# Fixed queue orders in the gradient pass, larger weight pieces at the hand-over, and the final parameter step in blocks

## Chip, cores and metric

One Trainium2 chip, one core. The time is the device time of one execution in microseconds, from three runs; the profile is of one more execution. PE is the matmul engine, DVE the vector engine, ACT the scalar engine, POOL GpSimd and SP the sync engine, which here only issues DMAs. ACT and POOL issue DMAs too, and each engine works through its own instructions in order: a DMA that has to wait on a semaphore holds up what stands behind it.

## What is computed

A layernormed input goes through a state-space convolution and is multiplied by the silu of a SwiGLU feed-forward; the kernel gives the output and the gradients by all inputs, L = 2048 rows, D = 576 channels, N = 128 states, F = 4608 hidden columns.

```python
xn = _layernorm(x)
s = _A_ref(xn, A_A_re, A_A_im, A_B_re, A_B_im, A_C_re, A_C_im, A_log_dt, A_Dskip)   # SSM convolution
h = silu(xn @ w1) * (xn @ w3); g = silu(h @ w2)
out = x + s * g
_out, _vjp = jax.vjp(_f, A_u, ..., B_w1, B_w3, B_w2); _grads = _vjp(grad_out)
```

out_0 is the output, out_1 the gradient by x, out_2 to out_9 those by the SSM parameters (out_8 by log_dt, 576 numbers), out_10 and out_11 by w1 and w3, out_12 by w2.

## The kernel before

A forward part (hidden columns, SSM, output) fills scratch tensors in DRAM: the gate values G, the up values U and spectra of the SSM (Q, PZ). `backward` then runs the **gradient pass**: 18 groups of 256 hidden columns (`FG`). For each, `phase6_load` brings two rows of w2 into one of four buffers on POOL (L1224), transposes them on SP to `w2T`, loads `gg_n` (G, L1229) and `h_n` (U, L1230) on POOL and prepares Silu (L1234) and its derivative (L1236) on ACT. `phase6_group` multiplies the output gradient by w2 (`ph`, L1259; its PSUM tiles are freed by ACT's copies `gh`, L1262) in four parts, with stages "h1" and "h3" after the second and fourth, stores GU and GG with SP, and goes on to the weight gradients: `phase6_grad2` (out_12, two a group, copies L1292) and `phase6_grad13` (out_10, out_11, copies L1309). The next group's tiles are loaded while a group runs; `gg_n` and `h_n` have two buffers each. A scheduler places the instructions on each engine by priorities (`at`).

Beside this, the SSM's backward convolution runs until about 1390 us; from group 11 on (`GP`) **parameter steps** (`param_step`, 72 of them, each half a chunk of 16 channels) are spread between the stages: SP loads `qT` and `gz`, ACT loads `pz` (L995), PE makes eight small matmuls into `et_ps` (three buffers), DVE multiplies (L1010) and reduces (L1013) into `S_all`. From there SP's order is the order of the code (`chain`).

At the **hand-over** the transposed weights w1 and w3 (36 blocks of 128 columns each) come in by SP as pieces, five transposes a piece (`load_piece`): 14 blocks of each early, the rest into buffers that the gradient pass gives back, then the transposed GG and GU rows (`acts`) of tiles 0 and 1. `phase6_inputs` makes the input gradient of 16 row tiles, 144 matmuls `px` each (L1348), adds on DVE (`gx`, L1355), and `ln_bwd_tile` goes back through the layernorm and stores out_1 (L1385). The remaining parameter steps stand at fixed stops in these tiles. `phase5_final` then turns `S_all` into out_2 to out_8, five chunks of channels: four PE transposes, some thirty DVE operations over 128 elements, and stores; out_8 goes out by elements at the end (L1096, L1098).

## Time and profile before

| | us |
|---|---|
| median of three runs | 2099.3 (2097.39 to 2102.25) |
| profiled execution / its span | 2097.32 / 2095.3 |
| PE busy | 1802.7 (86%) |
| DVE busy | 1401.2 (67%) |
| ACT busy | 881.0 (42%) |
| POOL busy | 278.9 (13%) |
| mean granted PE clock | 0.946 |

Stages in the span: the forward part up to about 840 us, the gradient pass to about 1640, the hand-over to about 1745, the input-gradient tiles to 2042, and the rest to 2095. The mean shares say little of a stage; a row of busy time for one stretch does. In rows of the time line a bracket holds the idle time of the engine ahead of the group and what ended it; "SPq" is SP's queue.

### The profile page before, as it was taken

The page shows a single profiled execution, that of the slowest core. Times are in us where ns is not written, and L with a number is a line of the kernel's source. Part 1 is how long each engine was busy: PE and PEld are TensorE (multiplying, and loading weights), DVE is VectorE, ACT ScalarE, POOL GpSimd, SP SyncE. Part 2 cuts the span into 40 slices and gives each one's busy share as a digit, 9 for nine tenths or more (in the row PEclk, how much of TensorE's full clock was granted, in tenths as well). Part 3 has the DMA queues.
Part 4 walks back from the last instruction along what each step waited for, and adds up shares of the span by engine and source line. Part 5 has one row for each costly group of instructions (what it writes and reads, how often), then busy time and mean ns, then how long its engine had stood idle before and what let it go on. Part 6 is the DMA issues. An engine that isn't in the chain of part 4 may idle for free. (4 is left out here: it accounts for less than half of the span.)

```text
span 2095.3 us, 40471 instructions
## 1 busy us (share of the span) xinstructions
PE 1802.7 (86%) x16538; PEld 1315.6 (63%) x16538; DVE 1401.2 (67%) x2283; ACT 881.0 (42%) x1612; POOL 278.9 (13%) x426
## 2 busy tenths in 40 slices
PE   1789999999997998899999998987797667998990
PEld 1444545455553676778787887876686545776880
DVE  7546565566884555396975979376697745787847
ACT  2967777775553111565656555445343100000000
POOL 5002222211113111111111111111110000000000
PEclk9999999999998999899999999998898888999995
DMA  3588777766659976547463756678789979999950
GB/s 79 209 310 284 263 261 254 268 236 234 204 171 256 222 188 176 178 149 204 144 189 113 204 160 203 180 180 202 195 216 186 209 141 208 203 217 192 214 129 20
DMA packets 625769, 411.24 MB, mean 196 GB/s; under 512 B 434160, under 2 KB 565360, under 8 KB 620976
## 3 DMA queue, kind: packets, MB, share of 16 engines
q1 hardware_dynamic: 566816, 272.26, 53.1%
q0 software_dynamic: 27792, 109.14, 15.5%
q10 hardware_dynamic: 30976, 27.27, 4.8%
q8 instruction: 129, 2.11, 0.4%
q14 instruction: 56, 0.46, 0.1%
HBM read 130.65 MB, written 185.65 MB: 151 GB/s over the span
## 5 line engine op out<-in xcount | busy, mean ns | idle before, releaser
L1348 PEld LDWEIGHTS <-acts 128*128 128x128 bf16 x2304 | 227.6, 100 | 93.6 <-DMA acts<-GU_dram 17.7
L1307 PEld LDWEIGHTS <-xn_bf 128*128 128x128 bf16 x2304 | 225.4, 98 | 33.9 <-issue 6.9
L1259 PE MATMUL ph<-w2T,goT 128*128 128x256 bf16 x1440 | 188.7, 285 | 66.2 <-ACT gh L1262 61.7
L1010 DVE TENSOR_TENSOR pr_q<-et_ps,pz 128x1024 f32<-128x1024 f32 x144 | 176.2, 1223 | 99.3 <-PE et_ps L1005 91.5
L1259 PEld LDWEIGHTS <-goT 128*128 128x128 bf16 x1440 | 144.7, 102 | 93.9 <-issue 65.4
L1348 PE MATMUL px<-wT,acts 128*128 128x288 bf16 x1408 | 181.9, 289 | 9.9 <-DMA wT<-in_B_w_dram 9.7
L1013 DVE TENSOR_REDUCE S_all<-pr_q 128x32 f32<-128x1024 f32 x144 | 175.3, 1217 | 3.5
L763 PE MATMUL pg<-wmB_w,xnT 128*128 128x512 bf16 x576 | 167.6, 382 | 3.8 <-ACT g_t L771 1.9
L763 PEld LDWEIGHTS <-xnT 128*128 128x128 bf16 x1152 | 104.7, 97 | 105.2 <-issue 19.3
L1288 PE MATMUL pgw<-go_o,h_n 128*128 128x288 bf16 x1152 | 158.3, 294 | 10.4 <-ACT gw L1292 10.4
L818 PE MATMUL po<-w2g,hc 128*128 128x288 bf16 x1152 | 148.6, 291 | 15.1 <-DMA w2g<-in_B_w_dram 14.9
L763 PE MATMUL pu<-wmB_w,xnT 128*128 128x512 bf16 x576 | 159.3, 380 | 0.5 <-ACT u_t L772 0.5
L767 ACT ACTIVATE s_t<-pg 128x512 bf16<-128x512 f32 x144 | 86.3, 599 | 145.1 <-PE pu L765 113.0
L1371 ACT ACTIVATE t<-gx 128x576 f32<-128x576 f32 x16 | 10.9, 683 | 315.0 <-DVE gx L1355 315.0
L818 PEld LDWEIGHTS <-hc 128*128 128x128 bf16 x1152 | 113.1, 99 | 47.1 <-issue 16.1
L1309 ACT CAST gw<-pgw 128x256 bf16<-128x256 f32 x144 | 54.2, 377 | 208.2 <-PE pgw L1307 188.1
L1288 PEld LDWEIGHTS <-h_n 128*128 128x128 bf16 x1152 | 115.3, 101 | 41.9 <-issue 11.2
L1348 PE MATMUL px<-wA,acts 128*128 128x288 bf16 x896 | 122.8, 297 | 20.4 <-DMA acts<-GU_dram 16.0
L1307 PE MATMUL pgw<-gu_n,xn_bf 128*128 128x256 bf16 x1152 | 133.2, 275 | 5.7 <-ACT gw L1309 4.4
L1307 PE MATMUL pgw<-gg_n,xn_bf 128*128 128x256 bf16 x1152 | 130.2, 273 | 0.0
L487 ACT ACTIVATE cs_k<-et_ps 128x512 bf16<-128x512 int16 x216 | 116.0, 640 | 6.6 <-PE et_ps L486 6.5
L777 POOL DMA_DIRECT2D G_dram<-g_t x72 | 52.6, 730 | 496.1 <-ACT g_t L771 477.2
(302 smaller groups left out, 3383.2 us busy)
## 6 DMA issues: line engine op xcount, KB each, us to landing
G_dram<-g_t POOLq DMA_DIRECT2D x72, 256.0 KB, 3.3
U_dram<-u_t POOLq DMA_DIRECT2D x72, 256.0 KB, 4.4
H_dram<-h_t SPq DMA_DIRECT2D x72, 256.0 KB, 3.4
Q_dram<-q_k SPq DMA_DIRECT2D x36, 512.0 KB, 3.2
gg_n<-G_dram POOLq DMA_DIRECT2D x18, 1024.0 KB, 5.8
h_n<-U_dram POOLq DMA_DIRECT2D x18, 1024.0 KB, 8.9
GU_dram<-gu_n SPq DMA_DIRECT2D x36, 512.0 KB, 4.3
GG_dram<-gg_n SPq DMA_DIRECT2D x36, 512.0 KB, 8.6
```

The source lines that it names most:

```text
L487: nc.scalar.activation(out=CS[:, :, o:o + 256], in_=pt[:].bitcast(I16)[:, :, 0::2], func=ACT.Sin, scale=6.283184 / 2 ** 16)
L763: nc.tensor.matmul(pt[:], lhsT=xnT[:, c, ts], rhs=wm[w][:, c, :], start=(c == 0), stop=False)
L767: nc.scalar.activation(out=s_t[:, :, q, :], in_=pgv, func=ACT.Silu)
L777: nc.gpsimd.dma_start(out=dst[fb * ng:(fb + 1) * ng, :, i0:i0 + NT, :].rearrange("g p t f -> p g (t f)"), in_=src[:].rearrange("p g t f -> ...
L818: nc.tensor.matmul(po_[:, pi_, 0:pw], lhsT=hc[:, fi, :], rhs=w2[fi][:, po:po + pw], start=(fi == 0), stop=(fi == FT - 1))
L1010: nc.vector.tensor_tensor(out=pr[:].rearrange("p r k e -> p r (k e)"), in0=T[h][:].rearrange("p k z d a -> p (k z d a)")[:, None].to_broad ...
L1013: nc.vector.tensor_reduce(out=self.S_all[:, :, d0:d0 + 4], in_=pr[:].rearrange("p r k (d a) -> p (r k) d a", d=4), op=ALU.add, axis=AX.X)
L1259: self.pe_last = nc.tensor.matmul(ph[j][:, k, :].rearrange("p (a f) -> p a f", f=P), lhsT=lw, rhs=rh, start=(n == 0), stop=(n == nfull))
L1288: self.pe_last = nc.tensor.matmul(pgw[pi_][:, 0:pw], lhsT=hn[:, tt, fl * P:(fl + 1) * P], rhs=go_o[:, tt, po:po + pw], start=(tt == 0), st ...
L1307: self.pe_last = nc.tensor.matmul(pw_[:, 0:FG], lhsT=self.xn_bf[:, tt, c * P:(c + 1) * P], rhs=nat[:, tt, :], start=(tt == 0), stop=(tt == ...
L1309: nc.scalar.copy(out=gw[:, c], in_=pw_[:, 0:FG])
L1348: self.pe_last = nc.tensor.matmul(px[pi_][:, 0:pw], lhsT=act[:, ai, fi, :], rhs=wT[ai][n][2][:, fi - f0, po:po + pw], start=(fi == 0 and a ...
```

## The change

Fixed orders: `after` makes an instruction follow the last one of its chain; `gp` does so for POOL's DMAs and `sc` for ACT's operations in the gradient pass. The w2 rows are loaded by SP, both rows of a group into one of two buffers, one group ahead; `h_n` is loaded two groups ahead at "h3"; Silu is issued at "h1", its derivative and the products at "h3"; the small remainders of out_10 and out_11 (`tail`) go behind the next `gg_n` load. The `pz` load is issued half a chunk earlier, apart from `qT` and `gz`.

Hand-over: 15 blocks of w1 and 13 of w3 come early, the rest in pieces of seven (and one of two); the four grad2 of the last two groups run ahead of the last grad13, with the piece loads between; GG of tile 1 is loaded ahead of the last two pieces, GU behind them, and step loads of the last group are held back (`hold`) until then. `phase6_inputs` takes the blocks in the order of the pieces and has steps at other stops, none in tile 0.

Final step: `phase5_blocks` takes five blocks of 64 (the last 32) channels of each half, in pieces that run at the stops as soon as the block's chunks are summed, with loads and stores on POOL, out_8 by elements after block 3 and block 4. `ln_bwd_tile` uses the `pr_q` buffer in place of its own.

```diff
+    def after(self, key, fn):
+        prev = self.last.get(key)
+        if prev is None:
             ins = fn()
         else:
-            with self.tc.issue_after(self.sp_last.ins):
+            with self.tc.issue_after(prev.ins):
                 ins = fn()
...
+    def sp(self, fn):
+        return self.after("sp", fn) if self.chain else fn()
+
+    def gp(self, fn):
+        return self.after("gp", fn)
+
+    def sc(self, fn):
+        return self.after("sc", fn)
 
...
         if dg == 1 and ch + 2 < nch:
-            self.loaded[ch + 2] = self.param_loads(ch + 2)
+            if self.hold is None:
+                self.loaded[ch + 2] = self.param_loads(ch + 2)
+            else:
+                self.hold.append(ch + 2)
         self.half += 1
+
+    def param_flush(self):
+        hold, self.hold = self.hold, None
+        for ch in hold:
+            self.loaded[ch] = self.param_loads(ch)
+            if (ch - 1) * 2 + 1 <= self.half:
+                self.param_load_p(ch)
+
...
-    def phase5_final(self, out, big, S_all, ps2):
...
+    def phase5_step(self, done):
+        if self.final_rows is None or done >= self.final_rows:
+            self.final_rows = next(self.final, 10 ** 6)
+
+    def phase5_blocks(self):
...
+        for j, c0 in enumerate(range(0, H, 64)):
+            R = min(64, H - c0)
+            v = slice(0, 2 * R)
...
+            sv = self.S_all[:].rearrange("p r (h c) -> p r h c", h=2)[:, :, :, c0:c0 + R]
+            sm = fp.tile([P, 4, 2, R], FP32, name="ST")
+            tt(out=sm[:, 0:2], in0=sv[:, 1:4:2], in1=sv[:, 4:8:2], op=ALU.subtract)
+            tt(out=sm[:, 2:4], in0=sv[:, 0:4:2], in1=sv[:, 5:8:2], op=ALU.add)
...
+            for k in range(2):
+                tt(out=Q[v, k, 0:2], in0=X[v, 2 + k:3 + k].to_broadcast([2 * R, 2, N]), in1=X[v, 0:2], op=ALU.mult)
+            tt(out=W[v, 0], in0=Q[v, 0, 0], in1=Q[v, 1, 1], op=ALU.subtract)
+            tt(out=W[v, 1], in0=Q[v, 0, 1], in1=Q[v, 1, 0], op=ALU.add)
+            yield 0
+            pt = self.ps_T.tile([P, 4, N], FP32, name="et_ps")
+            with self.tc.issue_after(self.pe_last.ins):
+                for k in range(4):
+                    nc.tensor.transpose(pt[v, k, :], sm[:, k].rearrange("p h c -> p (h c)"), self.ident_f[:])
...
+            yield 0
...
+            for k in range(2):
+                tt(out=Q[v, k], in0=ST[v, 2 * k:2 * k + 1].to_broadcast([2 * R, 4, N]), in1=X[v, 0:4], op=ALU.mult)
+            tt(out=O[v, 0:2], in0=Q[v, 0, 0:4:2], in1=Q[v, 1, 1:4:2], op=ALU.subtract)
+            nc.vector.scalar_tensor_tensor(out=O[v, 2:4], in0=Q[v, 0, 1:4:2], scalar=-1.0, in1=Q[v, 1, 0:4:2],
+                                           op0=ALU.mult, op1=ALU.subtract)
+            for k, on in enumerate(("out_6", "out_4", "out_7", "out_5")):
+                for h in range(2):
+                    nc.gpsimd.dma_start(out=aps[on][H * h + c0:H * h + c0 + R, :], in_=O[R * h:R * h + R, k])
+            yield 0
...
+            for k in range(2):
+                tt(out=Q[v, k, 0:2], in0=W[v, k:k + 1].to_broadcast([2 * R, 2, N]), in1=ST[v, 1:4:2], op=ALU.mult)
+            tt(out=ST[v, 1], in0=Q[v, 0, 0], in1=Q[v, 1, 1], op=ALU.subtract)
+            nc.vector.scalar_tensor_tensor(out=ST[v, 3], in0=Q[v, 0, 1], scalar=-1.0, in1=Q[v, 1, 0],
+                                           op0=ALU.mult, op1=ALU.subtract)
...
+            for k, (a, b) in enumerate(((ST[v, 1:4:2], X[v, 4:6]), (ST[v, 0:1], W[v, 0:1]), (ST[v, 2:3], W[v, 1:2]))):
+                nc.vector.tensor_tensor_reduce(out=Q[v, 1, 2:4] if k == 0 else Q[v, 1, 2:3], in0=a, in1=b, scale=1.0, scalar=0.0,
+                                               op0=ALU.mult, op1=ALU.add, accum_out=acc[v, k:k + 1])
+            tt(out=acc[v, 0:1], in0=acc[v, 0:1], in1=acc[v, 1:2], op=ALU.add)
+            tt(out=self.gl_bf[v, j:j + 1], in0=acc[v, 0:1], in1=acc[v, 2:3], op=ALU.subtract)
...
+            for ai, n in ((0, 15), (1, 13)):
+                wT.append((ai, 0, n, wA.tile([P, n, D], BF16, name=f"wA{ai}")))
...
-                nxt = self.phase6_load(gi + 1, T0 + TG * gi, TG, wp, inp) if gi + 1 < NG else None
+                lastg = gi == NG - 1
+                nxt = self.phase6_load(gi + 1, T0 + TG * gi, TG, wp, inp) if not lastg else None
+                prep = nxt[-1] if nxt else iter(())
+                if lastg:
+                    self.tail()
...
                 for stage in self.phase6_group(gi, cur, elp, gwp, ps_h, ps_gw):
-                    if stage in ("h1", "h3") and gi < NG - 2:
-                        w2(gi, stage == "h3")
-                    if stage == "h1" and gi == NG - 1:
-                        self.load_piece(wT, inp, "gg_n", ((0, FA, 7),))
-                        self.load_piece(wT, inp, "gu_n", ((1, FA, 7),))
-                        self.load_piece(wT, wp, "w2T", ((0, FA + 7, 2),))
+                    if stage in ("h1", "h3"):
+                        next(prep, None)
+                        if gi < NG - 2:
+                            w2(gi, stage == "h3")
+                        if stage == "h3" and gi + 2 < NG:
+                            self.phase6_load_h(gi + 2, T0 + TG * gi, inp)
+                    if stage == "h1" and lastg:
+                        self.load_piece(wT, inp, "gg_n", 0, 15, 7)
+                        self.load_piece(wT, inp, "gu_n", 1, 15, 7)
+                        self.load_piece(wT, wp, "w2T", 1, 13, 2)
                     if stage == "stored":
                         c = gi - GP
                         if 0 <= c < cfg.DT:
...
+                        if c in (1, 3):
+                            step()
...
-                            for fl in range(2):
-                                w2(gi - 1, fl)
+                            for g in (NG - 2, NG - 1):
+                                for fl in range(2):
+                                    w2(g, fl)
                                 step()
-                            self.load_piece(wT, wp, "w2T", ((1, FA + 7, 2),))
-                            self.load_piece(wT, inp, "h_n", ((0, FA + 9, 3), (1, FA + 9, 3)))
-                    elif gi >= GP:
+                                if g == NG - 2:
+                                    self.load_piece(wT, inp, "h_n", 1, 22, 7)
+                                else:
+                                    self.load_piece(wT, inp, "h_n", 0, 22, 7)
+                            acts.append(self.load_acts(1, (0,)))
+                    elif gi >= GP and not (lastg and stage in ("out_10", "end")):
                         step()
                 cur = nxt
-            for fl in range(2):
-                w2(NG - 1, fl)
-                step()
-            self.load_piece(wT, inp, "gg_n", ((0, FA + 12, 7),))
-            self.load_piece(wT, inp, "gu_n", ((1, FA + 12, 7),))
-            self.load_piece(wT, inp, "h_n", ((0, FA + 19, 3), (1, FA + 19, 3)))
-            for w in wT:
-                w.sort(key=lambda part: part[0])
-            acts.append(self.load_acts(1))
+            step()
+            self.load_piece(wT, inp, "gg_n", 0, 29, 7)
+            self.load_piece(wT, inp, "gu_n", 1, 29, 7)
+            self.load_acts(1, (1,), acts[1])
+            self.param_flush()
             ffn.close()
-            self.phase6_inputs(T2, TX, wT, acts)
-            while self.half < 2 * (D // 16):
-                self.param_step()
+            self.phase6_inputs(T2, TX, wT, acts, pool)
...
+    def phase6_load_h(self, gi, T, inp):
+        self.at(T)
+        hn = inp.tile([P, self.cfg.LT, self.FG], BF16, name="h_n")
+        self.gp(lambda: self.nc.gpsimd.dma_start(out=hn[:], in_=self.U_dram[gi]))
+        self.hn[gi] = hn
...
-            fi = gi * nfl + fl
-            w2r = self.w2rows[fi % len(self.w2rows)]
-            nc.gpsimd.dma_start(out=w2r[:, 0:D], in_=aps["B_w2"][fi * P:(fi + 1) * P, :])
-            self.nat_transpose(w2T[:, fl], w2r[:])
+            self.nat_transpose(w2T[:, fl], self.w2rows[gi % 2][:, fl])
+        if (gi + 1) * FG < cfg.F:
+            self.w2row_load(gi + 1)
         gg = inp.tile([P, LT, FG], BF16, name="gg_n")
-        hn = inp.tile([P, LT, FG], BF16, name="h_n")
         gu = inp.tile([P, LT, FG], BF16, name="gu_n")
-        nc.gpsimd.dma_start(out=gg[:], in_=self.G_dram[gi])
-        nc.gpsimd.dma_start(out=hn[:], in_=self.U_dram[gi])
+        self.gp(lambda: nc.gpsimd.dma_start(out=gg[:], in_=self.G_dram[gi]))
+        if self.tail:
+            self.tail()
+        self.tail = None
+        hn = self.hn[gi]
+        return w2T, hn, gg, gu, self.phase6_prep(hn, gg, gu)
+
+    def phase6_prep(self, hn, gg, gu):
+        nc, LT = self.nc, self.cfg.LT
         quarters = [slice(s * LT // 4, (s + 1) * LT // 4) for s in range(4)]
-        self.at(T + 0.4 * TG)
         for sl in quarters:
-            nc.scalar.activation(out=gu[:, sl, :], in_=gg[:, sl, :], func=ACT.Silu)
+            self.sc(lambda: nc.scalar.activation(out=gu[:, sl, :], in_=gg[:, sl, :], func=ACT.Silu))
+        yield
         for sl in quarters:
-            nc.scalar.activation(out=gg[:, sl, :], in_=gg[:, sl, :], func=ACT.Derivative_silu)
+            self.sc(lambda: nc.scalar.activation(out=gg[:, sl, :], in_=gg[:, sl, :], func=ACT.Derivative_silu))
         for sl in quarters:
             nc.vector.tensor_tensor(out=gg[:, sl, :], in0=gg[:, sl, :], in1=hn[:, sl, :], op=ALU.mult)
             nc.vector.tensor_tensor(out=hn[:, sl, :], in0=gu[:, sl, :], in1=hn[:, sl, :], op=ALU.mult)
-        return w2T, hn, gg, gu
...
-                stops = (6, 18, 30) if 0 < i and i % 2 == 0 else (8, 22)
-                for n in range(len(wT[0])):
-                    f0, f1 = wT[0][n][:2]
-                    for fi in range(f0, f1):
-                        for ai in range(2):
-                            for pi_, (po, pw) in enumerate(pieces):
-                                self.pe_last = nc.tensor.matmul(px[pi_][:, 0:pw], lhsT=act[:, ai, fi, :],
-                                                                rhs=wT[ai][n][2][:, fi - f0, po:po + pw],
-                                                                start=(fi == 0 and ai == 0),
-                                                                stop=(fi == FT - 1 and ai == 1))
-                        if fi in stops:
-                            self.param_step()
+                stops = () if i == 0 else (14, 38, 62) if i % 2 == 0 else (20, 50)
+                for n, (ai, fi, w) in enumerate(steps):
+                    for pi_, (po, pw) in enumerate(pieces):
+                        self.pe_last = nc.tensor.matmul(px[pi_][:, 0:pw], lhsT=act[:, ai, fi, :], rhs=w[:, po:po + pw],
+                                                        start=(n == 0), stop=(n == len(steps) - 1))
+                    if n in stops:
+                        self.param_step()
+                        self.phase5_step(self.half // 2)
```

On POOL, around the load of `gg_n` for a late group (before): out_dram<-gw rows are stores of weight gradients, w2r the w2 rows.

```order
L1293 DMA out_dram<-gw_19380 128x576
L1312 DMA out_dram<-gw_19412 128x4x256
L1312 DMA out_dram<-gw_19502 128x4x256
L1224 DMA w2r_10820<-in_B_w_dram 128x576
L1321 DMA out_dram<-gw13t 64x256
L1322 DMA out_dram<-gw13t 64x256
L1229 DMA gg_n<-G_dram 128x4096
L1224 DMA w2r_10821<-in_B_w_dram 128x576
L1293 DMA out_dram<-gw_19765 128x576
```

The same place on POOL after the change:

```order
L1356 DMA out_dram<-gw_19398 128x576
L1270 DMA h_n<-U_dram 128x4096
L1376 DMA out_dram<-gw_19428 128x4x256
L1376 DMA out_dram<-gw_19522 128x4x256
L1286 DMA gg_n<-G_dram 128x4096
L1388 DMA out_dram<-gw13t 64x256
L1389 DMA out_dram<-gw13t 64x256
L1356 DMA out_dram<-gw_19771 128x576
```

The w2 loads are gone from this queue, and `gg_n` stands directly behind the stores of the group before.

On SP, at the hand-over, the last weight pieces (wT_ and the first block's number) and tile 1's acts before the change:

```order
L1208 DMA_TRANSPOSE qT<-Q_dram 128x16x128
L992 DMA gz_13737<-gK_dram 64x1024 x2
L1208 DMA_TRANSPOSE wT_26_21719<-in_B_w_dram 128x7x128 x4
L1208 DMA_TRANSPOSE wT_26_21719<-in_B_w_dram 128x7x64
L1208 DMA_TRANSPOSE wT_26_21725<-in_B_w_dram 128x7x128 x4
L1208 DMA_TRANSPOSE wT_26_21725<-in_B_w_dram 128x7x64
L1208 DMA_TRANSPOSE wT_33_21731<-in_B_w_dram 128x3x128 x4
L1208 DMA_TRANSPOSE wT_33_21731<-in_B_w_dram 128x3x64
L1208 DMA_TRANSPOSE wT_33_21731<-in_B_w_dram 128x3x128 x4
L1208 DMA_TRANSPOSE wT_33_21731<-in_B_w_dram 128x3x64
L1208 DMA_TRANSPOSE acts<-GG_dram 128x36x128
L1208 DMA_TRANSPOSE acts<-GU_dram 128x36x128
```

And after it, from tile 0's GU on:

```order
L1265 DMA_TRANSPOSE acts<-GU_dram 128x36x128
L1265 DMA_TRANSPOSE wT_22_21361<-in_B_w_dram 128x7x128 x4
L1265 DMA_TRANSPOSE wT_22_21361<-in_B_w_dram 128x7x64
L1265 DMA_TRANSPOSE wT_22_21459<-in_B_w_dram 128x7x128 x4
L1265 DMA_TRANSPOSE wT_22_21459<-in_B_w_dram 128x7x64
L1265 DMA_TRANSPOSE acts<-GG_dram 128x36x128
L1265 DMA_TRANSPOSE wT_29_21684<-in_B_w_dram 128x7x128 x4
L1265 DMA_TRANSPOSE wT_29_21684<-in_B_w_dram 128x7x64
L1265 DMA_TRANSPOSE wT_29_21690<-in_B_w_dram 128x7x128 x4
L1265 DMA_TRANSPOSE wT_29_21690<-in_B_w_dram 128x7x64
L1265 DMA_TRANSPOSE acts<-GU_dram 128x36x128
```

Between tile 0's GU and tile 1's GU before has 35 piece transposes and three pairs of step loads (`qT`, `gz`), after 20 and none.

On DVE, the end of the program before:

```order
L1091 CAST gl_bf<-glogdt 128x5
L1082 TENSOR_TENSOR ft_25462<-ST,C_re_bf 64x128
L1085 TENSOR_SCALAR gout<-gr,dt_col 64x128
L1083 TENSOR_TENSOR gi<-gi,ft_25462 64x128
L1088 TENSOR_SCALAR gout<-gi,dt_col 64x128
```

And after:

```order
L1133 TENSOR_TENSOR acc_b<-acc_b 64x1
L1134 TENSOR_TENSOR gl_bf<-acc_b 64x1
L1424 TENSOR_TENSOR gx_25344<-px_25162,gxs_25164 128x288
L1424 TENSOR_TENSOR gx_25344<-px_25163,gxs_25164 128x288
L1447 ISA pr_q,mgx<-gx_25344,xn_bf 128x576
L1447 ISA mgx 128x1
L1450 TENSOR_SCALAR nmgx<-mgx 128x1
L1451 TENSOR_SCALAR pr_q<-xn_bf,nmgx,mg 128x576
L1452 TENSOR_TENSOR pr_q<-gx_25344,pr_q 128x576
L1453 SCALAR_TENSOR_TENSOR o_25348<-pr_q,rstd,go_25166 128x576
```

Before, the operations of `phase5_final` stand last; now the last block's sum for out_8 (`gl_bf`) stands ahead of the last tile's `gx`.

279 lines of the change are left out of this document (133 added, 146 removed).

## The prediction

> **What bounds the kernel now.** I first cut the profiled execution (2097.32 us, of which 2095.3 are its span) into stages: the view of busy time by stretches, one row each for the second part of the gradient pass, the hand-over, the sixteen input-gradient tiles and the end. Columns: stretch, its length, then busy us and instruction count of PE, PE's weight loads, DVE, ACT and POOL, the granted clock, the DMA engines' share, GB/s.
>
> ```profile
> 1400.00:1640.00 240.00, 194.49 (x1842) 165.88 (x1839) 184.09 (x199) 100.45 (x163) 28.14 (x47) 0.90 0.87 200
> 1640.00:1745.00 105.00, 58.63 (x438) 43.32 (x436) 51.61 (x49) 6.13 (x17) 4.26 (x7) 0.76 0.84 177
> 1745.00:2042.00 297.00, 284.90 (x2414) 227.89 (x2415) 210.20 (x272) 11.04 (x29) 0.00 (x0) 0.98 1.03 194
> 2042.00:2095.00 53.00, 1.76 (x15) 1.21 (x12) 38.32 (x223) 3.32 (x7) 0.00 (x0) 0.55 0.09 20
> ```
>
> PE bounds the first and third rows, with 46 us missing in the first. In the hand-over it works 59 of 105 us; at the end DVE works through small operations and nothing else runs. Three places can therefore give time. Next, the view of waits (who waited, for whom, us in total, times, longest), and the time line around one of the longest PE waits:
>
> ```profile
> POOL w2r L1224 <- DMA w2T<-w2r: 132.3, 17, 13.1
> PE ph L1259 <- ACT gh L1262: 61.7, 16, 14.1
> ACT gu_n L1234 <- DMA gg_n<-G_dram: 48.1, 7, 14.2
> ...
> 1409.73 2.89 PE L1259 MATMUL ph<-w2T,goT 128*128 128x256 bf16 x25
> 1411.96 0.56 POOL L1224 DMA_DIRECT2D w2r<-in_B_w_dram  x1 [10.63 <-DMA w2T<-w2r]
> 1413.58 0.57 POOL L1229 DMA_DIRECT2D gg_n<-G_dram  x1
> 1420.43 2.00 ACT L1234 ACTIVATE gu_n<-gg_n 128x1024 bf16<-128x1024 bf16 x2 [12.98 <-DMA gg_n<-G_dram]
> 1425.44 3.36 PE L1259 MATMUL ph<-w2T,goT 128*128 128x256 bf16 x15 [12.82 <-ACT gh L1262]
> ...
> 1515.59 3.36 PE L1259 MATMUL ph<-w2T,goT 128*128 128x256 bf16 x15 [14.05 <-ACT gh L1262]
> ...
> 1450.68 0.55 POOL L1229 DMA_DIRECT2D gg_n<-G_dram  x1 [0.70 <-PE pgw L1317]
> 1459.27 2.95 ACT L1234 ACTIVATE gu_n<-gg_n 128x1024 bf16<-128x1024 bf16 x3 [1.67 <-DMA gg_n<-G_dram]
> 1466.65 2.21 PE L1259 MATMUL ph<-w2T,goT 128*128 128x256 bf16 x10 [2.54 <-ACT gh L1262]
> ...
> 1578.80 0.55 POOL L1229 DMA_DIRECT2D gg_n<-G_dram  x1 [0.26 <-issue]
> 1597.73 1.06 ACT L1234 ACTIVATE gu_n<-gg_n 128x1024 bf16<-128x1024 bf16 x1 [13.75 <-DMA gg_n<-G_dram]
> 1599.31 4.28 PE L1259 MATMUL ph<-w2T,goT 128*128 128x256 bf16 x20 [14.13 <-ACT gh L1262]
> ...
> DMA to landing us min/median/max: 5.1/7.5/18.9
> ```
>
> Group 12 (around 1410) is a chain through three queues: POOL holds a load of a w2 row until its buffer has been transposed (10.63 us), the G load stands behind it, Silu behind that load, and behind Silu the copy that frees PSUM for PE. Group 14 (1515) repeats it. In group 13 no w2 load was ahead of the G load, which left as soon as its buffer was free: PE lost 2.54 us. Group 16 is different: its load left in time at 1578.80, but its data took 18.9 us (the last row: landing times of all 18 G loads) instead of 7.5.
>
> **The change, gradient pass.** With the w2 rows on SP, POOL has nothing ahead of the G load but stores of finished results. In groups 12 and 14 I put what is left at group 13's value, 2.5 us each: 12.82 + 14.05 - 5.0 = **-21.9**. Also 15 matmuls after such a gap take 3.36 us (0.224 each) against 0.116 in the row at 1409.73, so each long gap costs another 15 x 0.108 = 1.6 us: **-3.2**. Group 16 has no grad2 between its two halves, before and after, and the fixed ACT order puts four Silu pieces ahead of the copies, where the row at 1597.73 has one. With a landing of 7.5 us its gap is 14.13 - 11.4 + 3 x 1.0 = 5.7: **-8.4**. If the landing stays at 18.9, the gap is 17 (+2.9). Ends for these terms: +3 in all if no load comes sooner, -46 if all gaps vanish. I take the sum -33.5, near group 13's row. The two extra parameter steps (in groups 12 and 14) and the later w2 transposes at the start of the pass, which now wait for row loads on their own queue, I put at **+2** (0 to +4; no row shows them, but PE has the convolution's matmuls at the start).
>
> **The change, hand-over.** The SP queue's time line, then PE's second tile:
>
> ```profile
> 1626.45 20.70 SPq L1208 DMA_TRANSPOSE wT<-in_B_w_dram  x15
> 1659.31 5.25 SPq L1208 DMA_TRANSPOSE acts<-GG_dram  x1
> 1664.69 5.31 SPq L1208 DMA_TRANSPOSE acts<-GU_dram  x1
> 1674.88 20.21 SPq L1208 DMA_TRANSPOSE wT<-in_B_w_dram  x15
> 1702.34 30.18 SPq L1208 DMA_TRANSPOSE wT<-in_B_w_dram  x20
> 1737.39 5.71 SPq L1208 DMA_TRANSPOSE acts<-GU_dram  x1
> ...
> 1746.05 4.21 PE L1348 MATMUL px<-wA,acts 128*128 128x288 bf16 x17 [4.91 <-DMA acts<-GU_dram]
> ```
>
> From 1659.31 to 1743.10 SP issues without a pause, and PE's second tile waits for the last of it. So this queue is the bound, and what leaves it counts in full. A transpose's price follows from the three counts: the 15 hold five each of 7, 7 and 2 blocks (20.70), the next 15 of 2, 3, 3 (20.21), the 20 of 7, 7, 3, 3 (30.18); solved, 7 blocks take 1.53, 3 take 1.48, 2 take 1.07. After the acts of tile 0, before has 35 transposes (50.4 us), after 20 of seven blocks: 30.6. That is -19.8. The loads of parameter steps between (1670.00 to 1674.88 and 1695.09 to 1702.34: 12.1 us) are held back until after the acts of tile 1: -12.1, and they then stand ahead of tile 2's acts, and of the first step in tile 1, which can give back a few us. The four grad2 now run before grad13; PE is not the bound, so their order costs nothing, unless the seven-block piece in the h_n buffers is kept back by grad2 of group 17 (128 matmuls at 0.124). I take **-31**; ends -20 (if seven blocks cost 2.1 us; the nearest row above is acts, 36 blocks in 5.25) and -45 (tile 1 starts on its w1 half while GU is still on its way).
>
> **The change, tiles and end.**
>
> ```profile
> L1010 DVE TENSOR_TENSOR pr_q<-et_ps,pz 128x1024 f32<-128x1024 f32 x144 | 176.2, 1223 | 99.3 <-PE et_ps L1005 91.5
> L1013 DVE TENSOR_REDUCE S_all<-pr_q 128x32 f32<-128x1024 f32 x144 | 175.3, 1217 | 3.5
> ...
> 2030.42 10.94 PE L1348 MATMUL px<-wT,acts 128*128 128x288 bf16 x88
> 2041.27 0.82 DVE L1355 TENSOR_TENSOR gx<-px,gxs 128x288 f32<-128x288 f32 x2 [13.49 <-PE px L1348]
> 2042.81 0.28 DVE L1044 TENSOR_TENSOR grho<-Wr_c,ST 128x128 f32<-128x128 f32 x1
> 2043.97 0.75 DVE L1381 TENSOR_TENSOR t<-gx,t 128x576 f32<-128x576 f32 x1
> 2044.84 0.81 DVE L1383 SCALAR_TENSOR_TENSOR o<-t,rstd,go 128x576 bf16<-128x576 f32 x1
> 2079.47 0.39 SPq L1096 DMA_DIRECT2D out_dram<-gl_bf  x1
> ...
> out_dram<-o ACTq DMA_DIRECT2D x16, 144.0 KB, 5.0
> ...
> out_dram<-gl_bf SPq DMA_DIRECT2D x1, 1.0 KB, 14.2
> out_dram<-gl_bf SPq DMA_DIRECT2D x1, 0.1 KB, 13.7
> ```
>
> The end now: last px done at 2041.2, layernorm's operations until 2045.65, small operations until 2080.5, the element stores of out_8 landed about 2094.2, end 2095.3: 54.1 us. After the change nothing of the parameter gradients stands behind the last tile on DVE. What stays is 4.4 (gx and layernorm), 0.3 (issue), 5.0 (an out_1 store), 1.1: about 10.8; with a quiet store 8. I take 10 left: **-44**. It holds if block 4's last stores are down by then. They go out during tile 15, which takes PE 144 x 0.124 = 17.9 us; in it DVE spends 4.4 on tile 14's layernorm and about 4.5 on block 4, and POOL issues 14 stores of 0.57 (row at 1413.58), half of them beside DVE, so the last leaves some 5 us before the last px ends. Landing after 14 us it would end 9 us behind it, no later than the 10 taken. Ends -30 and -47.
>
> The Trainium skill (DMA: Bandwidth & Descriptors, Rules for kernel authors) says that a transfer whose last dimension isn't contiguous becomes one descriptor per element. The rows agree: 1 KB of out_8 takes 14.2 us, nearly three times a 144 KB out_1 store. The change keeps element stores, so by that rule their price isn't saved, only moved under matmuls; if the last of them left only behind the layernorm, the sum would be 9 us worse (14.2 instead of 5.0).
>
> In return DVE gets the blocks inside the tiles. One operation costs 0.28 us at 128 and 0.75 at 576 elements, so about 1.05 ns an element and 0.15 fixed (about half of it hidden back to back). A block has 19 operations (6 over 128 elements, 9 over 256, 2 over 512, 2 over one), 4096 elements in all: 4.3 + 1.3 to 2.8, say 6.3 us; five blocks 31. A step costs DVE 2 x (1.223 + 1.217) = 4.9, and 34 steps stand in tiles 1 to 14: 166; sixteen times gx and layernorm at 4.4 make 70. Sum 267 us against PE's 15 x 144 x 0.124 = 268 plus steps and transposes, near 285. So DVE fits on the whole, but three blocks fall into tiles 1 to 6, where both are equal. I take **+4** for this and the held loads (0 to +31, the blocks in full; below nothing by 4 if the acts, which make PE wait now, arrive earlier).
>
> **Sum.** -33.5 + 2 - 31 - 44 + 4 = -102.5: 2097.3 - 102.5 = 1994.8 for a profiled execution. That one lies 2 us under the median of the three runs (2099.3), so **1997 us**, own range 1978 to 2014.
>
> **Rivals.**
> *Loads stay late (15%).* Group 16's G load was on time and landed after 18.9 us all the same. If the wait is in the transfers and not in the queue, group 16 keeps its gap (+11: 2008), and with groups 12 and 14 too all 33.5 us fall away: 2031. For it: that row. Against: in groups 12 and 14 the load left late, in 13 it left on time and landed in 8.6. The Trainium skill (DMA: Bandwidth & Descriptors, Issuing engines are not separate DMA queues) is on this rival's side: DMAs from all engines share the same 16 DMA engines, and another issuer only saves issue time. The rows answer that here the issuer's queue itself stood 10.63 us.
> *DVE becomes the bound in the tiles (10%).* If each block stalls PE for its whole length, 31 instead of 4: 2024. For it: DVE and PE within a few per cent in tiles 1 to 6. Against: PE's queue runs a step ahead (three et_ps buffers).
> *The hand-over gives half (10%).* If a queue other than SP (ACT's pz load, behind which copies stand) ends last, -15 instead of -31: 2013.
> *Slower (5%).* The mechanism: ACT's fixed order lets no copy pass Silu, so in every one of the 17 groups a G load that lands late stops PE. At 7.5 us it costs about 2.5 us. Each us later costs 17 us. The gains of hand-over and end with the tiles' cost (-71) are eaten when it lands 4.2 us later, at 11.7; at 18.9 us in every group the kernel would take 2097 - 71 + 17 x 11.4 = 2220. Against: the median is 7.5, and in group 13 the copies already stood behind three pieces of Silu.
> *The change doesn't do what it says (5%)*: the scheduler leaves blocks or stores behind the last tile, and the end keeps 30 of its 44 us: 2027.
> The forecast itself has 55%. The range reaches up to the DVE and late-load cases, 2030, and down to the good ends of hand-over and tiles, 1975. A measurement of this kernel can tell about 0.2% (4 us) from no change; faster 0.94, within 0.02, slower 0.04.
>
> **What would show it.** In the profile after: POOL's waits for w2T gone from the view of waits; PE's waits for gh at groups 12 and 14 under 4 us; PE's second tile some 31 us nearer to the store of the last group; at the end 8 to 13 us between the last px and the end of the span, with an out_1 store landing last. It is wrong if Silu's wait for G grows in the sum (now 48.1 us in 7 groups), if PE waits for et_ps buffers in tiles 1 to 6 by more than 10 us, or if a POOL store ends the chain.

## The result, and the profile after

| | before | after |
|---|---|---|
| median (lowest to highest), us | 2098.35 (2094.08 to 2102.25), 4 runs | 2024.95 (2017.81 to 2026.19), 4 runs |
| ratio to before | | 0.9644 (95%: 0.9614 to 0.9673) |
| profiled execution / its span | 2097.32 / 2095.3 | 2026.19 / 2024.4 |
| start of the span to the first `ph` | 850.0 | 857.4 (+7.4) |
| gradient pass, first to last `ph` | 780.5 | 753.5 (-27.0) |
| hand-over, last `ph` to tile 2's first `px` | 135.8 | 102.0 (-33.8) |
| tiles 2 to 15, to the last `px` | 275.1 | 304.6 (+29.5) |
| last `px` to the end | 54.0 | 6.9 (-47.1) |

The change gains 73 us where 102 were forecast. The last five rows are differences of times in the two traces: the first `ph` and tile 2's first `px` by their start, the last `ph` and `px` by their end. Their changes add up to the difference of the spans (-71). One of them is far from the forecast: the tiles. The view of busy time by stretches, with the columns of before's, cut at the stages of after:

```profile
1400.00:1611.00 211.00, 186.47 (x1809) 160.39 (x1808) 187.18 (x199) 98.97 (x162) 24.20 (x40) 0.96 0.95 228
1611.00:1713.00 102.00, 79.28 (x631) 60.56 (x628) 46.92 (x51) 8.88 (x22) 13.27 (x24) 0.88 1.07 209
1713.00:2017.50 304.50, 271.14 (x2293) 216.85 (x2290) 239.51 (x349) 17.08 (x43) 57.46 (x112) 0.96 1.03 185
```

In the tiles (third row) PE misses 33 us of 304.5, where before, with tile 1 in its stretch, it missed 12 of 297. DVE is busy for 239.51, far from the whole stretch. The view of waits says what for:

```profile
PE ph L1322 <- ACT gh L1325: 19.0, 9, 7.6
...
DVE pr_q L1096 <- DMA X_b<-in_A_C_re_dram: 17.2, 2, 9.6
PE px L1417 <- DMA acts<-GG_dram: 17.1, 1, 17.1
...
PE et_ps L1031 <- DMA gz<-gK_dram: 12.7, 3, 8.2
```

POOL's wait for w2T is gone, and PE's wait for `gh` fell from 61.7 to 19.0. Three waits stand out: PE waits once for `acts` (17.1; before, 20.5 in six waits of at most 4.9), DVE twice for `X_b` (the block's parameters, 17.2; new), and PE three times for `gz` (12.7, of which 10.9 in the gradient pass; before, 15.4, all in the hand-over). The time line of POOL, DVE, SP and PE around the first two:

```profile
1738.73 2.06 POOL L1128 DMA_DIRECT2D out_dram<-X_b  x4 [3.65 <-ACT X_b L1125]
1750.66 1.03 POOL L1087 DMA_DIRECT2D X_b<-in_A_B_re_dram  x2 [9.87 <-DMA out_dram<-X_b]
...
1757.55 0.42 DVE L1096 TENSOR_TENSOR pr_q<-X_b 128x256 f32<-128x256 bf16 x1 [9.55 <-DMA X_b<-in_A_C_re_dram]
...
1797.73 0.76 DVE L1096 TENSOR_TENSOR pr_q<-X_b 128x256 f32<-128x256 bf16 x2 [7.67 <-DMA X_b<-in_A_C_re_dram]
...
1944.83 1.25 POOL L1138 DMA_DIRECT2D out_dram<-gl_bf  x2
...
1946.52 22.47 SPq L1265 DMA_TRANSPOSE acts<-GG_dram  x1
1969.03 11.65 SPq L1265 DMA_TRANSPOSE acts<-GU_dram  x1
...
1978.77 3.54 PE L1417 MATMUL px<-wA,acts 128*128 128x288 bf16 x14 [17.08 <-DMA acts<-GG_dram]
```

First cause: `X_b` has one buffer, and block 0 uses it at its end to stage out_2 and out_3. The next block's loads must wait until those stores are down, and DVE, which takes its operations in order, stands 9.55 us at the first one that reads them; the same again for block 2. Second cause: directly behind the element stores of out_8 (`gl_bf`, two of 64x4 elements, at 1944.83) SP's transpose of `acts` takes 22.47 us where those of the hand-over, below, take 4.5 to 6.4, and PE waits 17.08 us. The view of DMA from 1944 to 1963: its GB/s in 40 equal slices; two queues, SP's (q1) and POOL's (q0), with packets, MB and the time that the packets took as a share of the 16 DMA engines' time (over 100% where packets overlap); then transfers issued there with their KB and the us from issue to landing:

```profile
GB/s 256 185 134 225 292 281 311 178 124 81 46 27 34 44 23 17 10 8 17 27 11 6 12 9 10 9 8 3 3 13 18 78 84 95 52 15 39 113 99 91
...
q1 hardware_dynamic: 3804, 1.27, 117.2%
...
q0 software_dynamic: 192, 0.07, 1.6%
...
gxs<-GXN_dram ACTq DMA_DIRECT2D x1, 288.0 KB, 28.5
...
out_dram<-o ACTq DMA_DIRECT2D x1, 144.0 KB, 25.2
...
out_dram<-gl_bf POOLq DMA_DIRECT2D x2, 0.5 KB, 15.4
```

For some 11 us (23 of the slices of 0.475 us are under 50 GB/s) little moves, and transfers of all three issuing queues are late together. It is SP's packets that last, not POOL's: q0 fills 1.6% of the engines' time. The hand-over went as forecast, by SP's queue:

```profile
1639.19 5.91 SPq L1265 DMA_TRANSPOSE acts<-GG_dram  x1
1645.19 6.40 SPq L1265 DMA_TRANSPOSE acts<-GU_dram  x1
1651.76 13.91 SPq L1265 DMA_TRANSPOSE wT<-in_B_w_dram  x10
1665.71 5.40 SPq L1265 DMA_TRANSPOSE acts<-GG_dram  x1
1671.20 16.29 SPq L1265 DMA_TRANSPOSE wT<-in_B_w_dram  x10
1687.54 4.48 SPq L1265 DMA_TRANSPOSE acts<-GU_dram  x1
```

It issues without a pause for 52.8 us (1639.19 to 1692.02) where before it took 83.8. PE's first tile waits for the weight pieces up to the last one; its second starts right behind it, on its first w1 blocks, 2 us before its GU has landed (1694.19):

```profile
1687.53 0.28 PE L1417 MATMUL px<-wT,acts 128*128 128x288 bf16 x1 [1.60 <-DMA wT<-in_B_w_dram]
1689.07 3.20 PE L1417 MATMUL px<-wT,acts 128*128 128x288 bf16 x13 [1.25 <-DMA wT<-in_B_w_dram]
1692.06 5.58 PE L1417 MATMUL px<-wA,acts 128*128 128x288 bf16 x42
```

At the end an out_1 store is last:

```profile
2017.40 0.82 DVE L1424 TENSOR_TENSOR gx<-px,gxs 128x288 f32<-128x288 f32 x2 [8.71 <-PE px L1417]
2021.57 0.34 ACTq L1455 DMA_DIRECT2D out_dram<-o  x1
```

### The profile page after: what moved, and what is told of

Read it like the earlier page. It is cut to its first block, busy times and chain, and to the rows that moved or that the text cites. A ratio compares the mean times of both kernels' runs of the same rounds, so it can differ in the third digit from the quotient of the medians.

```text
span 2024.4 us, 40373 instructions
## 1 busy us (share of the span) xinstructions
PE 1785.9 (88%) x16465; PEld 1311.4 (65%) x16538; DVE 1392.8 (69%) x2142; ACT 888.7 (44%) x1624; POOL 324.3 (16%) x516
## 5 line engine op out<-in xcount | busy, mean ns | idle before, releaser
L1322 PE MATMUL ph<-w2T,goT 128*128 128x256 bf16 x1440 | 180.6, 278 | 21.7 <-ACT gh L1325 19.0
L1351 PE MATMUL pgw<-go_o,h_n 128*128 128x288 bf16 x1152 | 155.6, 291 | 10.9 <-ACT gw L1355 8.4
L773 PE MATMUL pg<-wmB_w,xnT 128*128 128x512 bf16 x526 | 158.0, 385 | 5.4 <-ACT g_t L781 2.6
L1417 PE MATMUL px<-wA,acts 128*128 128x288 bf16 x896 | 120.1, 294 | 17.1 <-DMA acts<-GG_dram 17.1
L1325 ACT CAST gh<-ph 128x512 bf16<-128x512 f32 x144 | 81.2, 610 | 81.7 <-PE ph L1322 55.1
```

Source lines behind the costliest of these rows:

```text
L773: nc.tensor.matmul(pt[:], lhsT=xnT[:, c, ts], rhs=wm[w][:, c, :], start=(c == 0), stop=False)
L1322: self.pe_last = nc.tensor.matmul(ph[j][:, k, :].rearrange("p (a f) -> p a f", f=P), lhsT=lw, rhs=rh, start=(n == 0), stop=(n == nfull))
L1325: self.sc(lambda: nc.scalar.copy(out=gh[:, j], in_=ph[j][:]))
L1351: self.pe_last = nc.tensor.matmul(pgw[pi_][:, 0:pw], lhsT=hn[:, tt, fl * P:(fl + 1) * P], rhs=go_o[:, tt, po:po + pw], start=(tt == 0), st ...
L1417: self.pe_last = nc.tensor.matmul(px[pi_][:, 0:pw], lhsT=act[:, ai, fi, :], rhs=w[:, po:po + pw], start=(n == 0), stop=(n == len(steps) - 1))
```

## The experiments

Theory A: the element stores of out_8 hold up all transfers behind them; that costs tile 13 its 17 us. Theory B: the second use of `X_b` costs tiles 4 and 5 theirs. The rival to both is that DVE has too much work in the tiles, as the prediction's second rival had it. Two more questions are which part of the change gives the gradient pass its gain, and what the extra and the held steps are worth. Times of single executions spread by some 10 us here, so stages are compared in the profiles beside the medians.

**Blocks 1 and 2 start one stop after their loads (blocks_later).**

```diff
             yield (c0 + R) // 8
+            if j in (1, 2):
+                yield 0
             sv = self.S_all[:]...
```

> Blocks 1 and 2 start one stop later than their loads, all else as in the changed kernel. Theory (DVE waits for the loads of X_b, 9.55 and 7.67 us, because one buffer serves all blocks): both waits fall under 2 us, tiles 4 and 5 (27.4 and 29.3 us) come near the 19 to 21 of their neighbours, and the kernel is 12 to 18 us faster than the changed one (2007 to 2013). Rival (DVE has too much work in tiles 1 to 6): the waits move but PE loses as much, the time stays within 4 us of 2025.

Measured: 2014.1 us (ratio 0.9594, 0.9569 to 0.9619). DVE's waits for `X_b` fell to 3.71 and 4.37 us, not under 2 as expected, and tiles 4 to 6 together from 77.6 to 69.0:

```profile
DVE pr_q L1098 <- DMA X_b<-in_A_C_re_dram: 8.1, 2, 4.4
```

A later use only shortens the wait: the load leaves no earlier. Tile 13 stays at 33.6 us: a separate cause, as A says.

**out_8 transposed by PE and stored in rows (out8_rows).** No element stores are left; the five columns are kept in f32, transposed at the end and stored by four row DMAs.

```diff
-                    for dst, src in self.block_vec(self.gl_bf, aps["out_8"], last=c0 + R == H and R < 64):
-                        nc.gpsimd.dma_start(out=src, in_=dst)
...
+                nc.tensor.transpose(pt[0:NB, 0, :], self.gl[:], self.ident_f[:])
+            nc.scalar.copy(out=self.gl_r[:], in_=pt[0:NB, 0, :])
...
+                nc.sync.dma_start(out=aps["out_8"][H * h:H * h + 64 * nb].rearrange("(j r) -> j r", r=64),
+                                  in_=self.gl_r[0:nb, 64 * h:64 * h + 64])
```

> out_8 goes out in rows of 64 and 32 numbers, after a PE transpose behind the last tile, instead of element by element; all else as in the changed kernel. Theory A (the element stores of out_8 behind block 3 hold up the transfers issued after them): the wait of 17.08 us for acts in tile 13 is gone, no acts load takes over 15 us to land there, and the kernel is 14 to 18 us faster (2007 to 2011); the end stays at 6 to 9 us behind the last px. Theory B (single slow transfers come by themselves, as the G load of 18.9 us in the kernel before): waits of such length stay, at this or another place, and the time stays within 5 us of 2025 in the middle of its runs.

Measured: 2018.22 us (0.965, 0.9586 to 0.9713; three runs of 2009.89 to 2021.70, one of 2041.53). Tile 13 takes 18.5 us and the end 7.2. The stretches of the old stall, with GB/s as the last column, and SP's queue there:

```profile
1925.00:1945.00 20.00, 20.00 (x178) 16.25 (x177) 18.82 (x27) 1.03 (x3) 4.13 (x8) 1.00 1.22 222
1945.00:1965.00 20.00, 20.00 (x174) 16.15 (x173) 19.11 (x29) 0.93 (x3) 8.10 (x16) 1.00 1.17 241
...
1951.14 6.08 SPq L1263 DMA_TRANSPOSE acts<-GG_dram  x1
1957.26 6.44 SPq L1263 DMA_TRANSPOSE acts<-GU_dram  x1
```

PE is busy all the time, and the transposes take 6 us. Tiles 4 and 5 keep their wait for `X_b` (11.00 and 8.64 in this execution). The median's interval is too wide to price the edit (14 to 18 us were expected); in the profile tiles 2 to 15 are 15.2 us shorter than in the change, and it shows the mechanism.

**Element stores once, behind block 4 (out8_once).**

```diff
-                if c0 + 128 > H:
-                    for dst, src in self.block_vec(self.gl_bf, aps["out_8"], last=c0 + R == H and R < 64):
+                if c0 + R == H:
+                    for dst, src in self.block_vec(self.gl_bf, aps["out_8"]):
```

> All element stores of out_8 go out together after block 4, in the last tile, none after block 3. Theory A (element stores hold up what is issued after them): tile 13's wait goes (-17) and comes back at the end, where the last out_1 store stands behind them: the end grows from 6.9 us to 12 to 25 us, the time is 2013 to 2028. Theory B (slow transfers come by themselves): tile 13 may keep its wait, the end grows by the landing time of the stores alone (about 14 us from their issue), 2025 to 2035.

Measured: 2025.86 us (0.9649, 0.958 to 0.9718), tile 13 34.5 us. The edit didn't do what it was meant to: the scheduler still issued the stores of the first four columns at 1936.99, and the stall stands behind them again. As the control it was to be, it is void; as one more case of stores and stall together, it agrees with A.

**Element stores early (elements_early).** As out8_rows, and in addition 64x4 elements of block 0 are stored twice, so that the same stores stand 200 us earlier; their content is written over by the row stores.

```diff
+            if j == 0:
+                self.gl_e = fp.tile([P, 4], BF16, name="gl_e")
+                nc.vector.tensor_copy(out=self.gl_e[:], in_=self.gl[:, 0:4])
...
+                    for dst, src in self.block_vec(self.gl_e, aps["out_8"], last=False):
+                        nc.gpsimd.dma_start(out=src, in_=dst)
```

> The kernel with out_8 in rows, and in addition two element stores of 64 x 4 numbers of out_8 right behind block 0 (written over by the rows at the end; they carry unfinished sums). Theory A (element stores hold up what is issued after them): the two stores take over 10 us to land, the transfers issued in the 10 us behind them (an acts transpose or step loads, in tiles 2 to 5) land only after them, 15 us and more after their issue where 5 to 10 is usual, and a wait of 8 to 18 us for acts, qT or gz shows on PE there; tile 13 stays without one. Theory B (slow transfers come by themselves, near tile 13): no such wait behind block 0, tiles 2 to 5 within 3 us of the kernel without these stores (19.4, 20.1, 29.0, 33.5).

Measured: 2012.58 us (0.9548, 0.943 to 0.9666, two runs). The time line of POOL, SP and PE, and the stretch:

```profile
1735.05 1.26 POOL L1142 DMA_DIRECT2D out_dram<-gl_e  x2
...
1740.17 19.83 SPq L1269 DMA_TRANSPOSE acts<-GU_dram  x1
...
1759.11 3.30 PE L1421 MATMUL px<-wA,acts 128*128 128x288 bf16 x13 [12.16 <-DMA acts<-GG_dram]
...
1735.00:1758.00 23.00, 10.93 (x93) 8.54 (x90) 7.00 (x8) 0.00 (x0) 5.02 (x11) 0.88 1.65 70
```

The stall moved with the stores: tile 3 takes 32.5 us (20.1 in after), tile 13 has none (19.1), and the DMA engines move 70 GB/s at full share. That settles A.

**Own tile for the staging of out_2 and out_3 (own_out_tile).**

```diff
-            nc.scalar.copy(out=X[v, 0:2], in_=ST[v, 1:4:2])
+            G = fp.tile([P, 2, N], BF16, name="G_b")
+            nc.scalar.copy(out=G[v], in_=ST[v, 1:4:2])
```

(and the two stores read `G` in place of `X`.)

> The changed kernel, where a block's out_2 and out_3 leave from a tile of their own instead of from X_b, so that the next block's loads don't wait for these stores. Theory (one buffer for all blocks, loads late by the landing of the stores): POOL's waits of 9.87 and 2.9 us for these stores ahead of the X_b loads go, DVE's waits for X_b (9.55 and 7.67 us) shrink by 5 to 10 us in the sum but not to nothing, since twelve issues of 0.52 us and a landing of 4 to 5 us stay; tiles 4 and 5 together 5 to 10 us shorter than 56.7. Rival (DVE has too much work there): tiles 4 to 6 stay at 75 to 80 us in the sum.

Measured: 2010.07 us (0.9536, 0.9418 to 0.9654, two runs). Block 1's wait fell from 9.55 to 3.38 us; block 2 still waits 7.55, now for a parameter that is loaded later (A_re). Tiles 4 to 6: 71.4 for 77.6. B holds, but neither edit for it takes the wait away alone.

**The w2 rows on SP, alone (w2_on_sp_alone).** The kernel before, with only the w2 rows moved: loaded by SP a group ahead into the four buffers, no fixed orders, nothing else of the change.

```diff
-            w2r = self.w2rows[fi % len(self.w2rows)]
-            nc.gpsimd.dma_start(out=w2r[:, 0:D], in_=aps["B_w2"][fi * P:(fi + 1) * P, :])
-            self.nat_transpose(w2T[:, fl], w2r[:])
+            self.nat_transpose(w2T[:, fl], self.w2rows[(gi * nfl + fl) % 4][:])
+        if (gi + 1) * FG < F:
+            self.w2row_load(gi + 1)
```

> The kernel before with one edit: the w2 rows are loaded by SP a group ahead (four buffers as before), no fixed orders. Theory (the w2 load in POOL's queue made the G load late in groups 12 and 14): PE's two gaps of 12.82 and 14.05 us fall to about 2.5 each, POOL's wait of 132 us for w2T is gone, and the kernel is 20 to 27 us faster than before (2071 to 2078), less 3 to 8 at the start of the pass, where the first rows now come by SP. Rival (the G loads are late for other reasons, the fixed orders did it): the gaps stay over 8 us, within 8 us of before.

Measured: 2085.35 us over ten runs (0.9925, 0.9898 to 0.9952). In the profile the gradient pass takes 748.7 us, 31.8 less than before and 4.8 less than after, and PE's wait for `gh`:

```profile
PE ph L1265 <- ACT gh L1268: 34.8, 15, 11.8
```

The gaps of groups 12 and 14 are gone with this edit alone; what is left is group 16 (11.8), whose G load took 16.5 us to land. The median gains 16 us, half of the 31.8 by which the profiled pass is shorter: that execution, at 2073.68, was the fastest of the ten.

**Without ACT's fixed order (free_act), without POOL's (free_pool).**

```diff
     def sc(self, fn):
-        return self.after("sc", fn)
+        return fn()
```

(in free_pool the same in `gp`.)

> The change without the fixed order of ACT's operations (Silu, its derivative and the copies of ph and of the weight gradients are placed by priorities again). Theory of the prediction: the fixed order puts four Silu pieces ahead of the copies that free ph, and costs up to 3 us in group 16 and nothing elsewhere: the gradient pass stays within 5 us of 753.5, the gap at 1580 (7.58) gets shorter by up to 3. Rival: the fixed order is what keeps Silu from standing ahead of the copies in the other groups; without it PE waits for gh again by 10 us or more in at least one group and the gradient pass is 10 us or more longer.

> The change without the fixed order of POOL's DMAs. Theory: what frees the G load is that the w2 rows have left this queue, not the order; the gradient pass stays within 5 us of 753.5 and no G load leaves more than 2 us after its buffer is free. Rival: without the order the h_n load (128x4096, two groups ahead) or stores that wait for copies stand ahead of the G load, which leaves 5 us or more later in some groups; PE then waits for gh by 10 us or more in sum beyond the 19.0 of the change, and the time is 2030 to 2040.

Measured: free_act 2033.47 us (0.9675, 0.963 to 0.972), free_pool 2023.44 (0.9618, 0.9577 to 0.9659). Without POOL's order the pass takes 752.7 us, the gap of group 16 7.02, the time is that of the change: the order is worth nothing that can be measured. Without ACT's order the pass took 766.3, and the gap of group 16 9.68 us with a G landing of 13.4; the rest lies in no single place. Against the change the median is 8.5 us higher, but the intervals of the two ratios overlap: what ACT's order is worth stays open, and nothing says that it costs time. For POOL the theory holds (a pass within 5 us of 753.5). For ACT it missed: the pass is 12.8 us longer, as the rival had it, though no single wait for `gh` reached the rival's 10 us.

**Without the two extra steps (no_extra_steps).**

```diff
-                        if c in (1, 3):
-                            step()
```

> The changed kernel without the two extra parameter steps in groups 12 and 14; two more steps stand in the last tile's end. Theory (the extra step of group 12 asks for gz before SP, behind two weight transposes, has brought it): PE's wait of 8.21 us for gz in group 13 and the 2.65 us in group 15 fall under 1.5 us, the gradient pass is 8 to 11 us shorter than 753.5. What it costs: two steps of 5 us DVE, with the last block behind them, at the end of the tiles, 5 to 25 us more at the end. Rival (gz is late by SP's queue alone): the waits stay at 6 us and more.

Measured: 2026.72 us (0.9615, 0.9466 to 0.9764, two runs). In the profile the pass is 7.9 us shorter (745.6), without PE's waits for `gz` of 8.21 and 2.65; the end is 13.5 longer (20.4), since the last steps and block 4 then stand behind the last `px`.

**Steps not held back (steps_not_held).**

```diff
-                            self.hold = []
...
-            self.param_flush()
```

> The changed kernel, where the step loads (qT, gz) of the last group are not held back until the weight pieces are issued. Theory (SP's queue sets the hand-over): SP still issues without a pause from the acts of tile 0 to those of tile 1, with two pairs of step loads (3.5 to 4.9 us each) in between; the time from the last ph to the start of tile 2 grows by 5 to 10 us over 102.0. Rival (PE's own work or the pieces' landing sets it): it stays within 3 us.

Measured: 2039.97 us (0.9678, 0.9559 to 0.9797, two runs). The hand-over took 107.3 us, 5.3 more than in the change. The pass was 13 us longer. It has a wait of 11.80 for `gz` at 1547, where the change waits 2.65 and no other profile over 4, just behind a G load that took 17.3 us to land; the difference of the medians isn't put down to the edit.

**All three edits (three_edits):** the diffs of blocks_later, out8_rows and own_out_tile in one kernel.

> out_8 by PE transpose and row stores, blocks 1 and 2 one stop later, and a tile of its own for the staging of out_2 and out_3, all in one. Theory A (element stores of out_8 hold up the acts of a later tile) and theory B (X_b loads wait for the stores of the block before) are two separate causes: their gains add. Then no PE wait over 5 us for acts or gz in any tile, DVE's waits for X_b together under 5 us, tiles 2 to 15 in at most 285 us (304.6 in the change), and the time 22 to 32 us under the change's 2025: 1993 to 2003. Rival: the loads of the blocks share a limit (the number of transfers at that time), what one edit frees the other loses again: tiles 2 to 15 at 290 or more and a time of 2006 to 2014, no better than the best single edit.

Measured: 1988.85 us (1985.32 to 2004.14, 6 runs), ratio 0.9476 (0.9438 to 0.9514) to before; 1993 to 2003 were expected. The profiled execution, at 2000.61, is 12 us above that median; its pass holds a late load that the last section shows. The gradient pass, hand-over, tiles and end by stretches:

```profile
1400.00:1619.00 219.00, 185.28 (x1797) 159.14 (x1795) 185.85 (x198) 98.65 (x161) 24.30 (x40) 0.95 0.97 218
1619.00:1719.00 100.00, 77.96 (x629) 59.80 (x627) 46.75 (x52) 8.61 (x22) 13.30 (x24) 0.90 1.06 216
1719.00:1991.70 272.70, 265.70 (x2293) 214.46 (x2291) 239.21 (x349) 17.09 (x43) 55.23 (x108) 0.99 1.08 206
1991.70:1998.80 7.10, 0.08 (x1) 0.00 (x0) 3.78 (x8) 1.03 (x3) 0.00 (x0) 0.69 0.07 21
```

Tiles 2 to 15 take 272.9 us, 31.7 less than in the change and 2 less than before, with the same DVE work (239.21 busy) as the change. Tiles 4 to 6 are 58.1 for 77.6, and the view of waits has no row of DVE for `X_b` any more. The two causes add: 15.2 us went with out8_rows alone, 31.7 with all three. The work itself is hidden. This kernel is faster than before and than the change, whose ratio is 0.9614 to 0.9673.

**The same without the extra steps (three_edits_no_steps).** The diffs of three_edits and no_extra_steps together.

> The same without the two extra parameter steps in groups 12 and 14. By the trace of the change without them alone the gradient pass loses its two gz waits (-8) and the end gets one step more behind the last tiles (+13). If that trade holds, the gradient pass is 6 to 9 us shorter than in the kernel with three edits, the end 8 to 14 longer, and the time within 7 us of it. Rival: the longer end came from the tiles' waits, which the three edits remove: then the end stays at 7 to 9 us and the time is 6 to 9 us lower.

Measured: 2009.39 us (1996.76 to 2018.74), ratio 0.9562 (0.9519 to 0.9604): 20 us slower than three_edits. The end takes 19.2 us for 7.2 and the pass 761.5 for 767.6, both as expected. But both passes hold late loads: this one a wait of 11.88 for `gz` and one of 16.02 in group 16, whose G load took 19.4 us to land. The profiled executions differ by 11 us, the medians by 20; the time isn't within 7 us, and the rest isn't explained. Here the extra steps are worth keeping; in the change, no_extra_steps shows no difference.

## Why the prediction was right in sign, inside its outer range alone, and 28 us off in size

The measured 2024.95 us lies outside the forecast's own range (1978 to 2014) and inside the wider one that takes in its rivals (1975 to 2030). The sum was -102.5, the span changed by -71.0. Of the 31.5 us between them the tiles make 25.5, the gradient pass with its start 11.9; hand-over and end gave 5.9 more than forecast.

- **Gradient pass: the reason right, the size not.** Groups 12 and 14 lost their gaps, and the w2 rows' move alone does it. Forecast -33.5 for the gaps and +2 for the extra steps and the start; measured -27.0 and +7.4. Group 16 kept 7.58 us (forecast 5.7) with a landing of 10.3. (The median of 7.5 us taken for a G load there was that of all the tile's transfers; for the 18 loads alone it is 5.8, minimum and maximum are the same.) The mis-sized part is "+2 (0 to +4)": behind the two extra steps PE waits 10.9 us for `gz`, and taking them out gave back 7.9. How much is owed to the steps stays open: free_pool keeps them and has no such wait in the pass, which is yet only 0.8 us shorter. At the start, PE's wait for `gs` grew from 3.90 to 7.92 us; w2_on_sp_alone has it too (8.53), so it comes with the loads on SP. The cause wasn't tried further, nor the remaining 3 us.
- **Hand-over: right.** -33.8 for -31. SP's queue was the bound, and 31.0 us left it. Tile 1 did start on w1 while GU was still on its way, as the good end of the range had it. A transpose of seven blocks took (13.91 + 16.29) / 20 = 1.51 us (forecast 1.53). The three prices solved from sums aren't those of single transposes, though: in before's trace one of 2, 3 or 7 blocks takes 1.24, 1.25 and 1.30 us in the median, and a few of 1.6 to 4.7 us make up the rest.
- **End: right.** -47.1 for -44, the good end of its range; 6.9 us left (10 forecast), an out_1 store last.
- **Tiles: the step that failed.** It counted DVE's instructions ("So DVE fits on the whole") and put +4 on blocks and held loads; measured +29.5. The count was near: the blocks keep DVE busy for 32.5 us (31 counted), and three_edits, with the same DVE work as the change, takes 2 us less than before. What it left out were the blocks' transfers. Two waits were missing from the sum: 17.2 us of DVE for `X_b` in tiles 4 and 5, and 17.1 of PE for `acts` in tile 13. One of the prediction's own signs of being wrong showed: PE waited 11.0 us for `et_ps` buffers in tiles 1 to 6, most of it right behind DVE's two waits for `X_b` (4.38 us at 1760.88, 3.13 at 1803.71). That the time fell into the wider range is luck: its upper end allowed the blocks' full length (+31, 2024 us), and two other waits came to nearly the same sum. The rival behind that end, that DVE's work itself stalls PE, is refuted by three_edits.
- **The element stores.** The prediction said of their price that it "isn't saved, only moved under matmuls", and asked only whether the last one leaves behind the layernorm. It took 14.2 us for the store's own price. The runs show that it is a price for every transfer behind it: before paid it at the end, when nothing else was under way. Under matmuls it fell on `acts`. The case that it did ask about didn't come: the last pair, of 32 elements each, landed 3.4 us after its issue. Before issued these stores on SP, the change on POOL; whether SP's would hold up others too, no run tried.
- **Loads stay late (rival): in part.** The late G load of group 16 before isn't a matter of queues. A load of 16.5 to 24.8 us came in w2_on_sp_alone, steps_not_held, three_edits and three_edits_no_steps too, in one or two groups of an execution, though nothing stood ahead of them on POOL. That another issuer changes little, as the rival has it, didn't hold in groups 12 and 14: there POOL itself had stood 10.63 us, and the move took that away.
- **Slower through ACT's fixed order (rival): no.** After's G loads landed in 5.1 to 10.3 us, below the 11.7 from which it would decide.

## What to carry to other kernels

When work moves from the end into a stage that is bound by PE, price its transfers as well as its instructions: which buffer a load waits for, and what else is under way when a store of single elements goes out. A buffer that is loaded first and used for staging at the end chains each block to the stores of the one before; a tile of its own or one stop of slack alone only shortened the waits, and in the kernel with both they were gone. And look for the one instruction that blocks an in-order queue: moving the w2 loads gave the pass its gain, the fixed order on POOL nothing.

## What the runs showed of the hardware

**Element stores hold up other queues.** Two stores of 64x4 two-byte elements, 1 KB in all, landed after 15.4 us in the change and 21.8 in elements_early. In that time the DMA engines are shown as busy at 79 or 70 GB/s, where out8_rows moves 241 in the same stage; in the change 256-byte packets of the transposes took up to 8.6 us each, with a median of 18 ns. The stores' own packets are short: the trace of the change has 32 of 32 bytes, from 1946.90 to 1948.27, of at most 25 ns each. Behind them others begin to last. Every one of the nine profiles with these stores in the tiles has a stretch of 10 us at 6 to 25 GB/s behind them, and PE waits there for 9 to 17 us; none of the three without them (out8_rows, three_edits, three_edits_no_steps) has it. The Trainium skill (DMA: Bandwidth & Descriptors, Queues, rings and completion order) says that each DMA engine takes turns between the queues it has work for, packet by packet. By that rule a 1 KB store would cost the others a few turns, which its packets show as short; the lateness behind them is measured all the same, and decides. Why the other queues' packets last that long stays open.

**Single loads land late without such a store.** In three_edits the G load of group 13 left on time and landed after 24.8 us; PE lost 13.71 (the landing times of its 18 G loads, from the view of their line; then the stretches ahead of that load and during it):

```profile
DMA to landing us min/median/max: 5.2/5.5/24.8
...
1428.00:1441.00 13.00, 12.29 (x135) 10.75 (x132) 12.56 (x13) 2.23 (x6) 1.54 (x2) 1.00 1.11 283
1441.00:1466.00 25.00, 12.50 (x107) 10.20 (x103) 12.97 (x13) 3.90 (x6) 1.63 (x3) 0.85 1.17 110
```

The rate falls from 283 to 110 GB/s, less deep than behind element stores. Five kernels' profiles have a G load over 16 us, at groups 13, 15 or 16. Such loads may be part of the 10 us by which executions of one kernel differ here (this one is 12 us above the median of its runs); their cause wasn't found.
